# Alternating the weight chunks of the first block by unit, and a new order of the tail's additions

## The chip, the cores and the metric

The kernel runs on one core of a Trainium2 chip. The metric is the time of one execution on the device in microseconds (us). TensorE (PE in the profile) multiplies, VectorE (DVE), ScalarE (ACT) and GpSimd (POOL) work elementwise, and SyncE (SP) issues every DMA of this kernel, in order, on one queue. Each engine takes its instructions strictly in the order in which the program issues them, and waits at an instruction until its inputs and its buffer are ready.

## What is computed

```python
def _A_ref(x, dft_seq_re, dft_seq_im, dft_hid_re, dft_hid_im):
    a = jnp.einsum("bsd,ed->bse", x, dft_hid_re)
    b = jnp.einsum("bsd,ed->bse", x, dft_hid_im)
    y = jnp.einsum("ts,bse->bte", dft_seq_re, a) - jnp.einsum("ts,bse->bte", dft_seq_im, b)
    return y

def _B_ref(x, w_gate, w_up, w_down):
    g = jnp.einsum("bsd,df->bsf", x, w_gate)
    u = jnp.einsum("bsd,df->bsf", x, w_up)
    h = _gelu(g) * u
    return jnp.einsum("bsf,fd->bsd", h, w_down)

h = x + _A_ref(_layernorm(x, axis=-1), A_dft_seq_re, A_dft_seq_im, A_dft_hid_re, A_dft_hid_im)
h2 = h + _B_ref(_layernorm(h, axis=-1), B_w_gate, B_w_up, B_w_down)
```

x has 2048 rows of 448; the feed-forward part is 1792 wide. All inputs are float32.

## The kernel before

Each float32 operand is split into a high and a low float16 half (`hi_part` on ACT, `lo_part` on DVE), and a product is made of three float16 products. Large products use a seven-product scheme for 2x2 blocks: sums and differences of the blocks are formed first (by DVE or POOL), seven products are accumulated in PSUM by PE, and the results are combined ("drained") afterwards.

**Stages.** The first 345 us are the Fourier sublayer (the sequence stage, `seq_mm` and `fast_mm`, with the hidden stage `hid_mm` between). Meanwhile ten of the fourteen gate/up weight chunks are prepared (`DFT_F` gives chunk and step) and stored in DRAM (`w_dram`); the chunks 0, 1, 2 come last and stay in the three-buffer ring of weights, `w_tile`. Then come 42 units t of the gate and up products (`GateUp`), in three blocks of `NF` = 14: block 0 covers half of the rows (512 columns of the moving side per matmul), blocks 1 and 2 a quarter each (256 columns). A unit makes the products `x1`, `z1` (issued at the end of the unit before), `y1`, `x2`, `z2`, `y2`, and `y3` (issued at the start of the unit after). They collect in three PSUM banks X, Y and Z. DVE makes the results: c from Z after `z2`, one half of the hidden values hs from Y after `y2` (L1019), the other half after `y3` (L1088). `y3` goes on in the bank that `y2` has filled, so PE waits there until DVE has read it.

**Block 0** also makes what the sequence stage had no time for. Four gate/up chunks (`JIT_F`, 3 to 6 before) are made just in time, two units ahead: four additions and four low halves on DVE (`w.sums`, `w.lo`), four high halves on ACT, and a store. In units 0 to 6 the seven chunks n of w_down are prepared (`down_hi`, `down_lo`, `down_sums`): their sums on POOL, three low halves on DVE. The remaining chunks are loaded back from `w_dram` two units ahead (`gw_load`). Units 6 and later also carry side work, lists of steps with a unit and a place k in it, run by `do(t, k)`: the split and transposition of the third quarter's activations (`AT_A`) and, in block 1, of the fourth's (`AT_B`).

**Blocks 1 and 2** also run the down product for what is ready: 56 chunks d = 7 p + n (row tile p of 8, chunk n of 7), each 21 matmuls (`dn_mm`). A chunk's hidden values are loaded from DRAM two units ahead (`hid_load`, six buffers), its sums are made at the end of that unit (`dn_sums`: two operations on POOL, the fifth sum on DVE), its high and low halves in the next unit (`dn_hi`, `dn_lo`), its matmuls in the one after. Chunks of the last two row tiles (`LAST`, p = 6 and 7) cannot all be run in the units; eight of them (`EARLY`: unit and chunk) are split beforehand, in units 32 to 41, at the end of the unit. When a row tile's seven chunks are done its four banks are drained (`Drain`): ACT copies two banks to v, DVE adds parts of all four, and POOL makes eight additions (`sums`) into hr, which is stored.

**The tail**, after unit 41, runs the chunks 42 to 52 and then the last three. The chunks in `jit` (46, 47, 48, 53, 54, 55) are still to be split; step i of the loop issues the split of one and the sums of the next. Drain 5's additions were issued at i = 5, drain 6 after chunk 48. Chunk 49's seventh product uses a bank that drain 6 has to release.

Of the kernel before, what the change touches and what calls it, by code (L numbers as in the profile page):

```python
# [13 lines left out]
P = 128  # L14
# [18 lines left out]
def kernel(  # L33
# [181 lines left out]

    def down_sums(n):
        t = wd32[n]
        s = wd_s[n] = fops.tile([P, 5, HD], F32, tag="xs", name=f"wd_s_{n}")
        G.tensor_sub(s[:, 2:4], t[:, 0:2], t[:, 2:4])  # L219
        t22 = t.rearrange("p (a b) d -> p a b d", a=2)  # L220
        G.tensor_add(s[:, 0:2], t22[:, :, 0], t22[:, :, 1])
        G.tensor_add(s[:, 4], t[:, 0], t[:, 3])
# [504 lines left out]


    gu = {}
    DFT_F = ((13, 17), (12, 20), (11, 25), (10, 29), (9, 33), (8, 37), (7, 41), (0, 45), (1, 48), (2, 50))  # L730
    JIT_F = range(3, 7)

    early, after = {}, {}

# [380 lines left out]
    def gw_load(t):  # L1115
        gw[t] = w_tile(f"gw{t}")
        nc.sync.dma_start(gw[t], w_dram[f_of(t)])
# [41 lines left out]
    def dn_sums(d):  # L1159
        t = dn_hid(d)  # L1160
        if d in LAST:
            spare.append(d)
            s = fops.tile([P, 5, P], F32, tag=("xn", "tt")[len(spare) % 2], name=f"dn_s{d}")
        elif d % 4 < 2:
            s = late.tile([P, 5, P], F32, tag="dn_s", bufs=2, name=f"dn_s{d}")
        else:
            if d % 4 == 2:
                opened["s"] = prep.tile([P, 10, P], F32, tag="s", name=f"dn_s{d}")
            s = opened["s"][:, d % 4 % 2 * 5 :][:, :5]
        dn_s[d] = s  # L1170
        G.tensor_add(s[:, 0:2], t[:, 0:2], t[:, 2:4])  # L1171
        G.tensor_sub(s[:, 2:4], t[:, 1:4:2], t[:, 0:4:2])  # L1172
        V.tensor_add(s[:, 4], t[:, 0], t[:, 3])  # L1173

    def dn_parts(d):
        return (dn_hid(d)[:, 0:4:3], slice(0, 2)), (dn_s[d], slice(2, 7))
# [68 lines left out]
    for q, t0, step, when in ((2, 6, 3, AT_A), (3, 14, 6, AT_B)):  # L1245
        for j in range(2):
            plan = (
                lambda q=q, j=j: ffn_bias(q, j),
                lambda q=q, j=j: ffn_norm_act(q, j, hp[q, j]),
                lambda q=q, j=j: ffn_sums(q, j, (0,)),  # L1250
                lambda q=q, j=j: ffn_sums(q, j, (1,)),
                lambda q=q, j=j: ffn_sums(q, j, (2,)),
                lambda q=q, j=j: ffn_hi(q, j, (0,)),
                lambda q=q, j=j: ffn_sums(q, j, (3,)),
                lambda q=q, j=j: ffn_lo(q, j, (0,)),
                lambda q=q, j=j: ffn_hi(q, j, (1,)),
                lambda q=q, j=j: ffn_lo(q, j, (1,)),
                lambda q=q, j=j: ffn_lo(q, j, (2,)),
                lambda q=q, j=j: ffn_lo(q, j, (3,)),
                lambda q=q, j=j: ffn_transpose(q, j, (0,)),  # L1260
                lambda q=q, j=j: ffn_lo(q, j, (4,)),
                lambda q=q, j=j: ffn_transpose(q, j, (1, 2)),
                lambda q=q, j=j: ffn_transpose(q, j, (3,)),
            )
            for (f, k), what in zip(when, plan):
                at(side, (t0 + step * j + f, k), what)
# [8 lines left out]
    cur = GateUp(0)  # L1275
    cur.x1()
    cur.z1()
    down_load(2)
    down_load(3)
    prev = None  # L1280
    for t in range(NF):
        w = gu.get(t + 2) if t + 2 in JIT_F else None
        if t + 2 > JIT_F[-1] and t + 2 < NF:
            gw_load(t + 2)
        elif t + 2 >= NF:
            gw_load(t + 2)
        if t + 2 == NF:
            for d in (0, 1, 2):
                hid_load(d)
        if t + 1 == NF:  # L1290
            hr_load(0)
        if prev:
            prev.y3()
        if w:
            w.sums()
        cur.y1()
        if t == 3:

            gelu_table()
        if w:  # L1300
            w.hi(True)
        if t < NC:
            down_hi(t, 0)
            down_lo(t, 0)
        cur.x2()
        if t < NC:
            down_hi(t, 1)
        if w:
            w.hi(False)
            w.lo(True)  # L1310
        cur.z2()
        do(t, 1)
        cur.y2()
        do(t, 2)
        cur.c_last()
        if t == NF - 1:
            dn_hi(0)
        if t == 1:
            hid_mm(NP - 1, 0)
        prev, cur = cur, GateUp(t + 1)  # L1320
        cur.x1()
        if w:
            w.lo(False)
            gw[t + 2] = w.w
        if t < NC:
            for part in W_LO1:
                down_lo(t, 1, part)
            if t + 1 < NC:
                down_sums(t + 1)
        if t == NF - 1:  # L1330
            dn_lo(0)
        cur.z1()
        if t == 1:
            hid_mm(NP - 1, 1)
            hid_add(NP - 1, 0)
            ffn_moments(NB - 1, 1, hp[NB - 1, 1], 0)
            hid.close()
            late = ctx.enter_context(tc.tile_pool(name="late", bufs=1, reuse_waits="tile"))
            hops_tile(2)
        if t == 2:  # L1340
            hid_add(NP - 1, 1)
            ffn_moments(NB - 1, 1, hp[NB - 1, 1], 1)
            h_store(NB - 1, 1)

            sd_last = root(moments[NB - 1, 1], "h_last")
        if t == 3:
            mv = moments[NB - 1, 1]
            moments[NB - 1, 1] = mv, rstd(mv, sd_last, "h_last", const)
        if t == NF - 2:
            dn_sums(0)  # L1350
        if t == NF - 1:
            dn_sums(1)
            dn_sums(2)
        do(t, 3)
        if t > 0:
            before.store()
        before = prev
        if w:
            w.store()
        if t + 4 in JIT_F and t > 0:  # L1360
            gu[t + 4] = Weights(t + 4)
        if 1 <= t and t + 3 < NC:
            down_load(t + 3)
        do(t, 4)


# [8 lines left out]
    for t in range(NF, N_GU):  # L1375
# [12 lines left out]
            hr_load(6 + (t == N_GU - 2))  # L1388
        dn_mm(now[0], range(0, 6))
        prev.y3()  # L1390
        cur.y1()
        cur.x2()
        dn_mm(now[0], range(6, 13 if len(now) == 1 else 21))
# [2 lines left out]
        cur.z2()  # L1396
        do(t, 1)
        cur.y2()
        do(t, 2)
        cur.c_last()  # L1400
        for d in ahead[:1]:
            dn_lo(d)
# [20 lines left out]
            dn_sums(d)  # L1423
        if extra is not None:
            dn_hi(extra)
            dn_lo(extra)
        do(t, 3)
        if t == NF:
            before.store()
# [11 lines left out]
    prev.y3()  # L1441
    hid_load(47)
    prev.store()
    drain = drains[5]
    jit = [46, 47, 48, 53, 54, 55]
    for i, d in enumerate(range(6 * NC, 7 * NC + 4)):
        dn_mm(d)
        if jit:
            n = jit.pop(0)
            dn_hi(n)  # L1450
            if jit:
                dn_sums(jit[0])
            dn_lo(n)
            if len(jit) > 1:
                hid_load(jit[1])
        if i == 5:
            drain.sums(range(8))
            dn_store(5)
        if d == 7 * NC - 1:
            drain = dn_drain(6)  # L1460
            drain.copy()
            drain.bank2()
            drain.bank3()
            drain.sums(range(8))
            dn_store(6)
# [73 lines left out]
```

## Time and profile before

| what | value |
|---|---|
| median of 3 runs | 732.19 us (730.95 to 733.11) |
| profiled execution | 733.34 us, of which the span is 730.6 us |
| granted clock of PE, mean | 0.991 |
| busy: PE, DVE, ACT, POOL | 709.9, 527.6, 355.6, 207.6 us |

The span runs from the first to the last instruction; the rest of the execution lies around it. Times in the views are microseconds from the start of the span. A line such as L1213 is a line of the kernel, and a helper's line can stand for many places: tiles tell them apart. A row of the timeline gives start, duration, engine, line, operation, tiles written and read, shapes and count; a bracket at its end is the engine's idle time just before it and who ended it.

### The profile page before, as it was taken

How to read it: one execution, taken by the hardware profiler on the slowest of the kernel's cores; microseconds unless marked ns; L12 is line 12 of the kernel's file. 1: busy time of each engine (PE TensorE's matmuls, PEld its weight loads, DVE VectorE, ACT ScalarE, POOL GpSimd, SP SyncE). 2: the span in 40 equal slices, each digit the busy share in tenths (PEclk: the TensorE clock that was granted, in tenths of full speed). 3: DMA queues.
4: the chain of work that ended last, by engine and by line, in shares of the span. 5: the costliest groups of instructions: out<-in, count | busy, mean ns of one | idle time of the engine just before them, and what ended most of it. 6: DMA issues, size and time to landing. Idle time of an engine off the chain costs nothing.

```text
span 730.6 us, 13052 instructions
## 1 busy us (share of the span) xinstructions
PE 709.9 (97%) x4952; PEld 483.5 (66%) x4952; DVE 527.6 (72%) x1024; ACT 355.6 (49%) x656; POOL 207.6 (28%) x240
## 2 busy tenths in 40 slices
PE   9999999999999999999998999999999999999868
PEld 5555555555555556988443344489998999899867
DVE  7996746677669689998769654467667856889872
ACT  5775524253425355542646544355555454555420
POOL 0000000000000000001234621244565764878762
PEclk9999999999999999999999999999999999999998
DMA  8887639999979689473738658894988867788312
GB/s 265 257 246 243 149 102 289 205 294 244 287 256 261 220 254 258 144 188 119 174 119 305 198 168 205 223 293 167 297 262 259 279 213 258 276 277 285 113 58 76
DMA packets 116463, 160.47 MB, mean 220 GB/s; under 512 B 62000, under 2 KB 80560, under 8 KB 116400
## 3 DMA queue, kind: packets, MB, share of 16 engines
q1 hardware_dynamic: 116400, 159.64, 72.8%
q8 instruction: 38, 0.62, 0.3%
q14 instruction: 25, 0.20, 0.1%
HBM read 110.85 MB, written 34.87 MB: 199 GB/s over the span
## 4 chain that ended last, share of the span: by engine, by line
PE 83%; DVE 7%; POOL 4%; DMA 3%; ACT 2%; issue 1%; SPq 0%; DVEq 0%; POOLq 0%; ACTq 0%
PE acc L647 32%; PE pY L1009 12%; PE acc_d L1213 11%; PE y L713 9%; PE pZ L1009 7%; PE pX L1009 7%; PE acc_f L519 6%; DMA hid<-hid_dram 2%; POOL hr L971 2%; DVE dn_w L112 1%; DVE gu_w L114 1%; POOL dn_s L1171 1%; POOL dn_s L1172 1%; DMA hid_dram<-hs 1%; DMA wr<-in_w_seq_dram 1%
## 5 line engine op out<-in xcount | busy, mean ns | idle before, releaser
L647 PE MATMUL acc<-xs,ws 128*128 128x448 f16 x1248 | 237.9, 352 | 0.2 <-ACT ws L108 0.2
L647 PEld LDWEIGHTS <-ws 128*128 128x128 f16 x1248 | 122.0, 98 | 114.2 <-ACT ws L108 0.4
L1009 PEld LDWEIGHTS <-gw 128*128 128x128 f16 x1365 | 133.3, 98 | 44.8 <-issue 1.9
L1213 PE MATMUL acc_d<-wd,dn_w 128*128 128x224 f16 x1008 | 110.6, 259 | 0.7 <-ACT v L939 0.7
L219 POOL TENSOR_TENSOR wd_s<-wd 128x448 f32<-128x448 f32 x7 | 7.9, 1131 | 347.4 <-DVE r_h L141 342.0
L1213 PEld LDWEIGHTS <-dn_w 128*128 128x128 f16 x1008 | 96.9, 98 | 2.8 <-issue 0.9
L1009 PE MATMUL pY<-hops,gw 128*128 128x256 f16 (+1 forms) x595 | 89.2, 294 | 0.0
L1103 POOL TENSOR_TENSOR hs<-hs,c 128x256 f32<-128x256 f32 (+1 forms) x42 | 52.8, 1257 | 126.5 <-DVE hs L1019 69.1
L114 DVE SCALAR_TENSOR_TENSOR ws<-wr,ws 128x1024 f16<-128x1024 f32 (+2 forms) x66 | 75.1, 1140 | 10.4 <-ACT ws L108 10.0
L108 ACT ACTIVATE ws<-wr 128x1024 f16<-128x1024 f32 (+2 forms) x66 | 63.8, 981 | 23.1 <-DMA wr<-in_w_seq_dram 21.5
L713 PE MATMUL y<-wh,z 128*128 128x448 f16 x336 | 66.2, 352 | 0.0
L1009 PE MATMUL pZ<-hops,gw 128*128 128x256 f16 (+1 forms) x385 | 61.7, 294 | 1.5 <-DVE c L1019 1.5
L1009 PE MATMUL pX<-hops,gw 128*128 128x256 f16 (+1 forms) x385 | 61.7, 294 | 0.0
L1171 POOL TENSOR_TENSOR dn_s<-hid 128x256 f32<-128x256 f32 x56 | 48.2, 861 | 34.9 <-DMA hid<-hid_dram 31.8
L112 DVE TENSOR_TENSOR dn_w<-dn_s,dn_w 128x640 f16<-128x640 f32 x48 | 54.1, 1127 | 0.1
L1019 DVE SCALAR_TENSOR_TENSOR c<-pZ,u 128x256 f32<-128x256 f32 (+1 forms) x42 | 21.4, 509 | 44.6 <-PE pZ L1009 42.2
L713 PEld LDWEIGHTS <-z 128*128 128x128 f16 x336 | 32.9, 98 | 30.1
L1009 PEld LDWEIGHTS <-gu_w 128*128 128x128 f16 x273 | 27.0, 99 | 38.9 <-issue 8.6
L1173 DVE TENSOR_TENSOR dn_s<-hid 128x128 f32<-128x128 f32 x56 | 30.8, 565 | 27.1 <-DMA hid<-hid_dram 26.8
L519 PEld LDWEIGHTS <-ws 128*128 128x128 f16 x504 | 48.3, 98 | 0.9
L1065 ACT ACTIVATE u<-pY 128x256 f32<-128x256 f32 (+1 forms) x42 | 19.1, 454 | 59.7 <-PE pY L1009 59.7
L1172 POOL TENSOR_TENSOR dn_s<-hid 128x256 f32<-128x256 f32 x56 | 45.1, 806 | 0.0
(133 smaller groups left out, 928.4 us busy)
## 6 DMA issues: line engine op xcount, KB each, us to landing
gw<-w_dram SPq DMA_DIRECT2D x35, 896.0 KB, 5.5
wr<-in_w_seq_dram SPq DMA_DIRECT2D x100, 256.0 KB, 4.7
hid_dram<-hs SPq DMA_DIRECT2D x28, 512.0 KB, 6.6
hid<-hid_dram SPq DMA_DIRECT2D x56, 256.0 KB, 5.9
w_dram<-gu_w SPq DMA_DIRECT2D x14, 896.0 KB, 6.0
gu_raw<-in_w_gu_dram SPq DMA_DIRECT2D x28, 384.0 KB, 5.8
wr<-in_w_seq_dram SPq DMA_DIRECT2D x14, 512.0 KB, 5.2
x<-in_x_dram SPq DMA_DIRECT2D x16, 224.0 KB, 3.9
```

What stands on the lines that cost most here:

```text
L108: A.activation(dst, src, AF.Copy, scale=scale)
L112: V.tensor_sub(dst, src, hi)
L114: V.scalar_tensor_tensor(dst, src, scale, hi, op0=ALU.mult, op1=ALU.subtract)
L519: PE.matmul(fast_sum(n, k), fast_a(n, i, lw, a), fast_b(j, lx, b), start=j == 0 and m == 0 and k % 2 == 0, stop=j == NT // 2 - 1 and m == ...
L647: PE.matmul(acc[key][:, :D], w[:, lw, block * P : (block + 1) * P], xs[c][:, lx, :], start=c == 0 and m == 0, stop=c == NT - 1 and m == 2,)
L713: PE.matmul(y[:, :D], z[p][:, lz, k, g * P : (g + 1) * P], wh[:, lw, k, :], start=k == 0 and m == 0, stop=k == 6 and m == 2,)
L1009: PE.matmul(ps, w[:, wl, wa + ws, :], ops[:, m + ms, :], start=first and n == 0, stop=last and n == len(terms) - 1, skip_group_check=True,)
L1103: G.tensor_mul(c22, c22, self.cols(self.c12))
L1171: G.tensor_add(s[:, 0:2], t[:, 0:2], t[:, 2:4])
L1172: G.tensor_sub(s[:, 2:4], t[:, 1:4:2], t[:, 0:4:2])
L1173: V.tensor_add(s[:, 4], t[:, 0], t[:, 3])
L1213: PE.matmul(ps, w[:, la, a, :], wd[n][:, lb, b, :], start=n == 0 and m == 0 and opens, stop=n == NC - 1 and m == 2, skip_group_check=True,)
```

## The change

- `DFT_F`, `JIT_F`: the sequence stage prepares the chunks 13, 12, 11, 9, 7, 5, 3, 0, 1, 2 (before: 13 to 7 and 0, 1, 2), block 0 makes 4, 6, 8, 10 (before: 3 to 6), in the units 2, 4, 6, 8. Chunks 3, 5, 7, 9 and 11 to 13 are loaded back.
- `PREP_AT`: down chunk n is prepared in the units 0, 1, 3, 5, 7, 9, 11 (before: 0 to 6). Its raw loads and its sums move with it; the sums of chunks from 2 on lie in another buffer, which the down product's sums use later as one tile of two halves.
- The fifth sum of a chunk becomes `dn_sum5`, issued after `y3` in the unit of its split, and in the tail after the low half of the chunk before.
- The low half of an `EARLY` chunk is issued a unit later, after `y3`. The last of them, 52's, stands in the tail.
- `do(t, 2)` in blocks 1 and 2 moves from behind `y2` to the end of the unit; one transposition moves to the next entry of the side list.
- In the tail hid 48 is loaded ahead of the loop, 53 to 55 a step earlier, and drain 5's additions and its store stand at i = 0, behind the sums of chunk 47.

```diff
@@ -215,7 +215,8 @@
 
     def down_sums(n):
         t = wd32[n]
-        s = wd_s[n] = fops.tile([P, 5, HD], F32, tag="xs", name=f"wd_s_{n}")
+        place = (late, "dn_s") if n > 1 else (fops, "xs")
+        s = wd_s[n] = place[0].tile([P, 5, HD], F32, tag=place[1], name=f"wd_s_{n}")
         G.tensor_sub(s[:, 2:4], t[:, 0:2], t[:, 2:4])
         t22 = t.rearrange("p (a b) d -> p a b d", a=2)
         G.tensor_add(s[:, 0:2], t22[:, :, 0], t22[:, :, 1])
@@ -727,8 +728,8 @@
 
 
     gu = {}
-    DFT_F = ((13, 17), (12, 20), (11, 25), (10, 29), (9, 33), (8, 37), (7, 41), (0, 45), (1, 48), (2, 50))
-    JIT_F = range(3, 7)
+    DFT_F = ((13, 17), (12, 20), (11, 25), (9, 29), (7, 33), (5, 37), (3, 41), (0, 45), (1, 48), (2, 50))
+    JIT_F = range(4, 11, 2)
 
     early, after = {}, {}
 
@@ -1162,7 +1163,9 @@
             spare.append(d)
             s = fops.tile([P, 5, P], F32, tag=("xn", "tt")[len(spare) % 2], name=f"dn_s{d}")
         elif d % 4 < 2:
-            s = late.tile([P, 5, P], F32, tag="dn_s", bufs=2, name=f"dn_s{d}")
+            if d % 4 == 0:
+                opened["l"] = late.tile([P, 10, P], F32, tag="dn_s", name=f"dn_s{d}")
+            s = opened["l"][:, d % 4 * 5 :][:, :5]
         else:
             if d % 4 == 2:
                 opened["s"] = prep.tile([P, 10, P], F32, tag="s", name=f"dn_s{d}")
@@ -1170,7 +1173,10 @@
         dn_s[d] = s
         G.tensor_add(s[:, 0:2], t[:, 0:2], t[:, 2:4])
         G.tensor_sub(s[:, 2:4], t[:, 1:4:2], t[:, 0:4:2])
-        V.tensor_add(s[:, 4], t[:, 0], t[:, 3])
+
+    def dn_sum5(d):
+        t = dn_hid(d)
+        V.tensor_add(dn_s[d][:, 4], t[:, 0], t[:, 3])
 
     def dn_parts(d):
         return (dn_hid(d)[:, 0:4:3], slice(0, 2)), (dn_s[d], slice(2, 7))
@@ -1259,8 +1265,8 @@
                 lambda q=q, j=j: ffn_lo(q, j, (3,)),
                 lambda q=q, j=j: ffn_transpose(q, j, (0,)),
                 lambda q=q, j=j: ffn_lo(q, j, (4,)),
-                lambda q=q, j=j: ffn_transpose(q, j, (1, 2)),
-                lambda q=q, j=j: ffn_transpose(q, j, (3,)),
+                lambda q=q, j=j: ffn_transpose(q, j, (1,)),
+                lambda q=q, j=j: ffn_transpose(q, j, (2, 3)),
             )
             for (f, k), what in zip(when, plan):
                 at(side, (t0 + step * j + f, k), what)
@@ -1275,14 +1281,12 @@
     cur = GateUp(0)
     cur.x1()
     cur.z1()
-    down_load(2)
-    down_load(3)
     prev = None
+    PREP_AT = {0: 0, 1: 1, 3: 2, 5: 3, 7: 4, 9: 5, 11: 6}
     for t in range(NF):
         w = gu.get(t + 2) if t + 2 in JIT_F else None
-        if t + 2 > JIT_F[-1] and t + 2 < NF:
-            gw_load(t + 2)
-        elif t + 2 >= NF:
+        n = PREP_AT.get(t)
+        if t > 0 and w is None:
             gw_load(t + 2)
         if t + 2 == NF:
             for d in (0, 1, 2):
@@ -1293,18 +1297,20 @@
             prev.y3()
         if w:
             w.sums()
+        if t == NF - 1:
+            dn_sum5(0)
         cur.y1()
         if t == 3:
 
             gelu_table()
         if w:
             w.hi(True)
-        if t < NC:
-            down_hi(t, 0)
-            down_lo(t, 0)
+        if n is not None:
+            down_hi(n, 0)
+            down_lo(n, 0)
         cur.x2()
-        if t < NC:
-            down_hi(t, 1)
+        if n is not None:
+            down_hi(n, 1)
         if w:
             w.hi(False)
             w.lo(True)
@@ -1322,11 +1328,13 @@
         if w:
             w.lo(False)
             gw[t + 2] = w.w
-        if t < NC:
+        if n is not None:
             for part in W_LO1:
-                down_lo(t, 1, part)
-            if t + 1 < NC:
-                down_sums(t + 1)
+                down_lo(n, 1, part)
+        if t + 1 in PREP_AT and t > 0:
+            down_sums(PREP_AT[t + 1])
+        if t == 0:
+            down_sums(1)
         if t == NF - 1:
             dn_lo(0)
         cur.z1()
@@ -1357,10 +1365,10 @@
         before = prev
         if w:
             w.store()
-        if t + 4 in JIT_F and t > 0:
-            gu[t + 4] = Weights(t + 4)
-        if 1 <= t and t + 3 < NC:
-            down_load(t + 3)
+        if w and w.f + 4 in JIT_F:
+            gu[w.f + 4] = Weights(w.f + 4)
+        if n is not None and 2 <= n + 2 < NC:
+            down_load(n + 2)
         do(t, 4)
 
 
@@ -1388,6 +1396,12 @@
             hr_load(6 + (t == N_GU - 2))
         dn_mm(now[0], range(0, 6))
         prev.y3()
+        for d in ahead:
+            dn_sum5(d)
+        if t - 1 in EARLY:
+            dn_lo(EARLY[t - 1])
+        if t in EARLY:
+            dn_sum5(EARLY[t])
         cur.y1()
         cur.x2()
         dn_mm(now[0], range(6, 13 if len(now) == 1 else 21))
@@ -1396,7 +1410,6 @@
         cur.z2()
         do(t, 1)
         cur.y2()
-        do(t, 2)
         cur.c_last()
         for d in ahead[:1]:
             dn_lo(d)
@@ -1423,7 +1436,7 @@
             dn_sums(d)
         if extra is not None:
             dn_hi(extra)
-            dn_lo(extra)
+        do(t, 2)
         do(t, 3)
         if t == NF:
             before.store()
@@ -1441,6 +1454,9 @@
     prev.y3()
     hid_load(47)
     prev.store()
+    hid_load(48)
+    dn_sum5(46)
+    dn_lo(52)
     drain = drains[5]
     jit = [46, 47, 48, 53, 54, 55]
     for i, d in enumerate(range(6 * NC, 7 * NC + 4)):
@@ -1451,11 +1467,13 @@
             if jit:
                 dn_sums(jit[0])
             dn_lo(n)
-            if len(jit) > 1:
-                hid_load(jit[1])
-        if i == 5:
-            drain.sums(range(8))
-            dn_store(5)
+            if jit:
+                dn_sum5(jit[0])
+            if len(jit) > 2:
+                hid_load(jit[2])
+            if i == 0:
+                drain.sums(range(8))
+                dn_store(5)
         if d == 7 * NC - 1:
             drain = dn_drain(6)
             drain.copy()
```

## The prediction

> **What bounds the kernel now.** I read the page first, then TensorE's own waits, then the timeline around each of those waits. The page:
>
> ```profile
> span 730.6 us, 13052 instructions
> PE 709.9 (97%) x4952; PEld 483.5 (66%) x4952; DVE 527.6 (72%) x1024; ACT 355.6 (49%) x656; POOL 207.6 (28%) x240
> ```
>
> PE is busy for 97% of the span and the change touches no matmul, so all that can be won lies in PE's few idle stretches and in slowed matmuls right behind them. The waits of PE (total, times, longest):
>
> ```profile
> PE acc_d L1213 <- ACT v L939: 7.0, 2, 6.3
> PE pY L1009 <- DVE hs L1019: 4.5, 2, 2.9
> PE acc_d L1213 <- DVE hs L1088: 2.0, 1, 2.0
> PE pZ L1009 <- DVE c L1019: 1.5, 2, 1.3
> ```
>
> That is 15.0 us, nearly all in six places. The timeline has them; the bracket is PE's idle time just before the row:
>
> ```profile
> 391.91 2.53 PE L1009 MATMUL pY<-hops,gu_w 128*128 128x512 f16 x11 [1.56 <-DVE hs L1019]
> 403.43 4.22 PE L1009 MATMUL pY<-hops,gu_w 128*128 128x512 f16 x11 [2.94 <-DVE hs L1019]
> 552.15 0.73 PE L1213 MATMUL acc_d<-wd,dn_w 128*128 128x224 f16 x6 [0.72 <-ACT v L939]
> 625.72 0.82 PE L1009 MATMUL pZ<-hops,gw 128*128 128x256 f16 x6 [1.30 <-DVE c L1019]
> 689.79 3.95 PE L1213 MATMUL acc_d<-wd,hops 128*128 128x224 f16 x24 [2.03 <-DVE hs L1088]
> 712.00 0.72 PE L1213 MATMUL acc_d<-wd,hops 128*128 128x224 f16 x3 [6.30 <-ACT v L939]
> ```
>
> Two lie in the first block, two in the middle, two in the tail. Three of them cost more than the idle time. Windows of the trace behind them (length, PE busy, weight loads, DVE, ACT, POOL, granted clock):
>
> ```profile
> 403.80:407.20 3.40, 3.40 (x10) 1.22 (x8) 2.68 (x5) 0.64 (x2) 3.40 (x2) 0.51 0.57 226
> 690.50:694.00 3.50, 3.50 (x22) 2.88 (x20) 1.46 (x2) 0.74 (x1) 0.44 (x1) 0.51 0.41 154
> 711.00:714.40 3.40, 2.40 (x14) 1.94 (x14) 0.00 (x0) 1.09 (x2) 3.32 (x6) 0.51 0.25 95
> 714.40:717.90 3.50, 3.50 (x22) 2.87 (x19) 0.00 (x0) 0.00 (x0) 3.24 (x6) 0.51 0.10 39
> ```
>
> After the idle stretches of 2.94, 2.03 and 6.30 us the clock was 0.51 for one, one and two windows of 3.4 us; a busy window at 0.51 loses 3.4 x 0.49 = 1.7 us. After 1.56 and 1.30 us I find no such window.
>
> **Part one, the first block.** A unit there takes PE 430.53 - 422.11 = 8.42 us (chain of waits, start and length):
>
> ```profile
> 422.11 2.37 PE pY L1009 x11
> 430.53 2.37 PE pY L1009 x11
> ```
>
> DVE's work for it stands in windows over 346 to 407 us of tile gu_s (four units' gate/up sums and their low halves: DVE, then ACT), of tile wd (five down chunks: PE, DVE, ACT, POOL), and in DVE's groups by form:
>
> ```profile
> 346.00:407.00 61.00, 16.27 (x24) 4.68 (x8) 0.97 0.61 191
> 346.00:407.00 61.00, 0.00 (x0) 11.10 (x15) 8.49 (x10) 12.35 (x14) 0.97 0.61 191
> L114 DVE SCALAR_TENSOR_TENSOR gu_w<-gu_raw,gu_w 128x512 f16<-128x512 f32 x4 | 2.7, 682 | 0.0
> L114 DVE SCALAR_TENSOR_TENSOR gu_w<-gu_raw,gu_w 128x256 f16<-128x256 f32 x4 | 1.7, 416 | 0.0
> L1019 DVE SCALAR_TENSOR_TENSOR c<-pZ,u 128x512 f32<-128x512 f32 x14 | 9.6, 689 | 20.9 <-PE pZ L1009 20.9
> ```
>
> A gate/up chunk costs DVE 16.27/4 + 0.68 + 0.42 = 5.17 us, a down chunk 11.10/5 = 2.22, the unit's own three results 3 x 0.69 = 2.07. With both chunks that is 9.46 us against 8.42: DVE falls back by about 1 us per unit, and by units 3 and 4 the second result (hs L1019) comes too late for the matmuls that go on in its bank. After the change no unit has both: 5.17 + 2.07 = 7.24 or 2.22 + 2.07 = 4.29 us. Nothing else is late next: units 6 to 12 also carry the split of the third quarter's activations, which now meets gate/up chunks 8 and 10, but in the one unit that has most of it (8) this is a few short instructions, and the result that PE needs stands ahead of them in DVE's queue. So both stalls and the slow window go: 1.56 + 2.94 + 1.7 = **6.2 us**. The work is not less, only spread. What was covered and may come out: weights 3 and 5 now come back from memory where 3 and 5 were made on the spot. Seven such loads stand in the block before and after, but the one for unit 5 joins the thickest traffic. From the page and the windows (the last two columns are the DMA share and GB/s):
>
> ```profile
> gw<-w_dram SPq DMA_DIRECT2D x35, 896.0 KB, 5.5
> 387.60:397.70 10.10, 8.54 (x40) 3.79 (x39) 9.34 (x16) 7.90 (x16) 3.56 (x3) 1.00 1.04 359
> ```
>
> It is issued on SP near 386, behind stores of hidden values, of h and of weights and behind a raw load, and lands after 5.5 us at the median. Unit 5's first matmuls come near 396 without the stalls (403.43 - 2.94 - 1.56 = 398.9, less two products of 1.3). If it stood last of all that this window moved, it would land at 397.7, 1.7 us late. I take nothing, the median being nearer, and keep 0 to 1.7 us.
>
> **Part two, the middle.** The two smaller stalls and what stood ahead of them:
>
> ```profile
> 550.29 1.08 ACT L108 ACTIVATE xs<-tt 128x768 f16<-128x768 f32 x2
> 622.58 0.29 DVE L1173 TENSOR_TENSOR dn_s<-hid 128x128 f32<-128x128 f32 x1 [1.33 <-DMA hid<-hid_dram]
> 622.78 0.95 DVE L112 TENSOR_TENSOR hops<-hid,hops 128x256 f16<-128x256 f32 x1
> 623.66 1.34 DVE L112 TENSOR_TENSOR hops<-dn_s,hops 128x640 f16<-128x640 f32 x1
> ```
>
> At 552 the drain's copy was behind 1.08 us of activation halves on ACT; the second side list now stands at the unit's end, behind the copy, so 0.72 us goes. At 625 DVE first sat 1.33 us for a transfer that its fifth addition needed, then did 0.95 + 1.34 us of an early chunk's low half, and only then the results that PE waited for. Now the results of the last matmuls come first, then the additions of chunks that have long landed, the low half, and the addition that may wait. The same work still stands ahead of c, but the 1.33 us of waiting gets filled: I take 1.0 of the 1.30. Sum **1.7 us**. Bounds: 0 (all of it comes back at another unit) to 2.0. The later low half holds a hid buffer longer, so one load (chunk 45's) goes out some 2 us later on SP; its sums come third in POOL's row there, so I cost it at nothing.
>
> **Part three, the tail.** It is the hard part. Rows of the timeline:
>
> ```profile
> 685.20 1.61 DVE L943 SCALAR_TENSOR_TENSOR hr<-acc_d,hr 128x224 f32<-128x224 f32 x4
> 668.92 4.04 POOL L971 TENSOR_TENSOR hr<-hr,v 128x224 f32<-128x224 f32 x4
> 689.48 0.73 POOL L1171 TENSOR_TENSOR dn_s<-hid 128x256 f32<-128x256 f32 x1 [0.76 <-DVE dn_xs L112]
> 697.77 6.20 PE L1213 MATMUL acc_d<-wd,dn_w 128*128 128x224 f16 x63
> 697.27 0.83 POOL L1171 TENSOR_TENSOR dn_s<-hid 128x256 f32<-128x256 f32 x1 [6.33 <-DMA hid<-hid_dram]
> 698.08 0.90 POOL L1172 TENSOR_TENSOR dn_s<-hid 128x256 f32<-128x256 f32 x1
> 699.01 0.74 ACT L108 ACTIVATE dn_w<-dn_s 128x640 f16<-128x640 f32 x1 [1.43 <-POOL dn_s L1172]
> 706.38 0.74 ACT L108 ACTIVATE dn_w<-dn_s 128x640 f16<-128x640 f32 x1 [1.01 <-POOL dn_s L1172]
> 706.31 11.33 POOL L971 TENSOR_TENSOR hr<-hr,v 128x224 f32<-128x224 f32 x16
> 711.41 0.54 ACT L939 ACTIVATE v<-acc_d 128x448 f32<-128x448 f32 x1 [4.29 <-POOL hr L971]
> 712.00 15.37 PE acc_d L1213 x129
> ```
>
> Before, POOL idles 6.33 us up to 697.27, does the sums of chunks 48, 53, 54, 55, and only from 706.31 drain 5's eight additions; ACT's copy of drain 6 waits for six of them until 711.41, PE until 712.00. On the same clock the new order runs so (to read against the rows):
>
> - The last result (hs L1088, for which PE waited until 689.79) no longer queues behind chunk 52's low half and follows the drain's additions, near 687.6. PE's 2.03 us there and the slow window at 690.5 go. PE then takes 2.0 us per chunk and is through 47 near 698.
> - DVE: fifth addition, then 52's low half (0.95 + 1.34): done near 690.2. POOL's sums of 47 share its buffer and wait for it, as at 689.48: 690.2 + 0.83 + 0.90 = 691.9.
> - Drain 5's eight additions now: the first six took 706.31 to 711.41, 0.85 us each, so 6.8 us: 698.7. Alone the later ones took (11.33 - 5.1)/10 = 0.62; four beside DVE's low halves 4.04, 1.01 each.
> - **What is late next** is chunk 48: its sums stand behind them on POOL, 698.7 + 1.73 = 700.4, then ACT and DVE, 0.74 + 1.34: 702.5. PE wants it at 698.5 and stops some 4 us. A second wait follows: drain 6's copy stands on ACT behind the high halves of 53, 54, 55. From the half of 48 to that of 55 it was 706.38 - 699.01 = 7.37 us, as DVE has 2.3 us of low half for each. So 700.4 + 7.4 + 0.74 = 708.5, and PE goes on 0.6 us later, 709.1 instead of 712.0: **2.9 us**.
> - From there the same 129 matmuls, 15.37 us with two slow windows behind the stall. At 2.0 us per 21 they are 12.3 us. With stalls of about 4 and 3.6 us instead of one of 6.3 I leave the slow windows as they are.
> - SP: the store of drain 5 waits for POOL and holds back the loads of 54 and 55; with 700 and a landing of 3 to 6 us they come when POOL reaches them or up to 3 us later. I take nothing.
>
> Bounds of the tail: additions at 1.01 give 1.3 us less, 1.6 us; the loads late by 3 us give 0. Additions at 0.62 (5.0 us) let PE go on at 707.3, and with full clock it ends 12.3 us later at 719.6 instead of 727.4: 7.8 us.
>
> **The sum.** 6.2 + 1.7 + 2.9 = 10.8 us. The profiled execution took 733.34 us (span 730.6 and 2.7 around it), so its like would take 722.5. It stands 1.15 us above the median of 732.19, so the median goes to **721.4 us**.
>
> The Trainium skill, "TensorE: Matmul & The Clock Gate", Part 1: The HAM clock gate, says that the clock halves after at least one idle window of about 3.4 us. By that, the stalls of 2.94 and 2.03 us would cost no clock and the sum would be 9.1 us, 723.1; the rows at 403.8 and 690.5 say otherwise, so I keep 1.7 for the first.
>
> **Rivals.**
>
> - *The tail is freed*: the 7.8 us of the upper bound, and chunks 53 to 55 at PE's own 2.0 us each instead of 7.37 / 3, 1.4 more: 6.2 + 1.7 + 9.2 = 17.1, 715.1 us. For: POOL had 6.33 idle us. Against: 0.95 and 1.34 us for low halves beside POOL.
> - *Transfers and POOL eat part of it*: unit 5's weights 1.7 us late, the middle 0, the tail 1.6: 4.5 + 1.6 = 6.1, 726.1 us. For: DMA share 1.04 there.
> - *The change doesn't do what it says*: the late hs in the first block is held by its buffer's store, not by DVE's load; then 6.2 stays, 4.6 is left, 727.6 us. Against: both rows of the stall name DVE, which worked without a pause there.
> - *Slower*: early chunks' low halves (2.29 us) stand ahead of the result c in seven units (33, 34, 36, 38 to 41), and PE waits for c in each as at 625. At 1.30 us each, 9.1, it takes the other 9.1 us back; from 1.6 us each it is slower beyond what a measurement of this kernel can tell (0.3%, 2.2 us), and at 2.03 each, 14.2 us, the time is 732.2 - 9.1 + 14.2 = 737.3. Against: before, the same instructions stood ahead of c, and one unit stalled by over 1 us.
>
> **Chances.** Forecast (719 to 724) 0.58; tail freed 0.15; part eaten 0.15; not what it says 0.05; slower mechanism 0.07, of which 0.04 beyond 0.3%. Something between forecast and no change may also land within 0.3%. So faster 0.90, same 0.06, slower 0.04. The range runs from the freed tail, 715.0, to 727.6.
>
> **What would show it.** Right: no PE idle before pY in units 3 and 4 and clock 1.00 at 390 to 410; no wait for hs L1088 at the start of the tail; POOL's eight additions before 48's sums; PE stalls at chunk 48 and at 49's seventh product, the latter behind ACT's high half of 55. Wrong: PE waits for gw in unit 5, for c in units 33 to 41, or no stall at 48 at all.

## The result, and the profile after

The changed kernel takes 719.82 us (median of 4 runs, 717.73 to 720.45) against 732.28 us (4 runs, 730.95 to 733.11) before: ratio 0.9827, 95% interval 0.9800 to 0.9853. Of the changed kernel's four runs the profiled one is the fastest, 717.73 us, and the only one with a granted clock of 1.000; the other three had 0.998, about one slow window of 3.4 us, and spans of 717.4 to 718.6 us. Its span is 14.6 us shorter than the span before (730.6 us), some 2 us more than the medians differ by.

The page and the waits of PE (total, times, longest), after the change:

```profile
span 716.0 us, 13066 instructions
PE 704.2 (98%) x4952; PEld 480.7 (67%) x4952; DVE 522.1 (73%) x1024; ACT 355.5 (50%) x656; POOL 201.9 (28%) x240
...
PE acc_d L1219 <- ACT v L940: 3.1, 1, 3.1
PE acc_d L1219 <- DVE dn_w L112: 2.3, 2, 1.4
...
PE pZ L1010 <- DVE c L1020: 1.2, 3, 0.6
```

The 4.5 us of pY on hs and the 2.0 us of hs at the tail's start are gone; the drain's copy costs 3.1 instead of 7.0. New is a wait of 1.4 us on a low half. The timeline of PE has these places:

```profile
389.55 1.24 PE L1010 MATMUL pY<-hops,gw 128*128 128x512 f16 x5
...
397.97 1.24 PE L1010 MATMUL pY<-hops,gu_w 128*128 128x512 f16 x5
...
481.00 0.56 PE L1219 MATMUL acc_d<-wd,dn_w 128*128 128x224 f16 x4 [1.40 <-DVE dn_w L112]
...
545.30 0.74 PE L1219 MATMUL acc_d<-wd,dn_w 128*128 128x224 f16 x6
...
618.21 0.82 PE L1010 MATMUL pZ<-hops,gw 128*128 128x256 f16 x6 [0.63 <-DVE c L1020]
...
692.73 0.37 PE L1219 MATMUL acc_d<-wd,dn_w 128*128 128x224 f16 x2 [0.40 <-ACT dn_w L108]
694.00 1.42 PE L1219 MATMUL acc_d<-wd,dn_w 128*128 128x224 f16 x13 [0.91 <-DVE dn_w L112]
...
700.22 0.45 PE L1219 MATMUL acc_d<-wd,hops 128*128 128x224 f16 x3 [3.08 <-ACT v L940]
```

Rows without a bracket had no wait. Both kernels issue 4952 matmuls of the same shapes in the same order, so the start of one matmul can be compared with its start before, and the change of that difference from place to place says where the 14.6 us between the two spans came from:

| matmul, start before and after | ahead by | since the row above |
|---|---|---|
| before the block, 349.41 and 348.99 | 0.42 | |
| end of the slow window in the block, 407.27 and 400.12 | 7.15 | +6.73: stalls 1.72 and 3.10, clock 1.69, rest 0.22 |
| start of block 1, 486.58 and 481.00 | 5.58 | −1.57: the new wait |
| drain 4's bank, 552.15 and 545.30 | 6.85 | +1.27 |
| c, 625.72 and 618.21 | 7.51 | +0.66 |
| last units, 678.50 and 672.17 | 6.33 | −1.18: waits for c and small ones |
| start of the tail, 689.79 and 681.23 | 8.56 | +2.22: no wait for hs |
| behind its slow window, 693.90 and 683.73 | 10.18 | +1.62: clock |
| chunk 48, 702.57 and 694.00 | 8.56 | −1.62: two waits |
| chunk 49's seventh product, 712.00 and 700.22 | 11.78 | +3.22: shorter wait |
| last matmuls, 727.10 and 712.49 | 14.61 | +2.83: clock |

That is 6.7 us from the block, −1.6 behind it, +0.7 from the middle and 8.3 from the tail. The first 0.42 us stand ahead of the block and are in none of these parts: at 349 us PE waits for ACT, 0.70 us before, not at all in this trace, and up to 1.10 us in others. That no slow window follows the tail's stall is seen in the windows (length, PE busy, weight loads, DVE, ACT, POOL, granted clock), two in the block and two behind the wait of 3.08 us:

```profile
389.60:393.00 3.40, 3.40 (x17) 1.52 (x16) 3.30 (x10) 1.41 (x3) 0.26 (x1) 1.00 1.09 403
397.97:401.40 3.43, 3.43 (x17) 1.55 (x16) 1.29 (x2) 1.40 (x3) 3.29 (x4) 1.00 0.63 207
...
700.20:703.60 3.40, 3.38 (x36) 3.37 (x36) 1.78 (x5) 0.41 (x1) 3.27 (x5) 1.00 0.00 0
703.60:707.00 3.40, 3.40 (x38) 3.40 (x36) 0.00 (x0) 0.00 (x0) 1.96 (x4) 1.00 0.14 54
```

The clock is 1.00 in all four, where three of the corresponding four before had 0.51.

### The profile page after: what moved, and what is told of

Read it like the earlier page. It is cut to its first block, busy times and chain, and to the rows that moved or that the text cites. A ratio compares the mean times of both kernels' runs of the same rounds, so it can differ in the third digit from the quotient of the medians.

```text
span 716.0 us, 13066 instructions
## 1 busy us (share of the span) xinstructions
PE 704.2 (98%) x4952; PEld 480.7 (67%) x4952; DVE 522.1 (73%) x1024; ACT 355.5 (50%) x656; POOL 201.9 (28%) x240
## 4 chain that ended last, share of the span: by engine, by line
PE 92%; DVE 4%; POOL 1%; DMA 1%; issue 1%; ACT 0%; SPq 0%; ACTq 0%; POOLq 0%; DVEq 0%
PE acc L648 33%; PE pY L1010 13%; PE acc_d L1219 12%; PE y L714 9%; PE pX L1010 9%; PE pZ L1010 9%; PE acc_f L520 7%; DVE dn_w L112 1%; DMA hid_dram<-hs 1%; DVE dn_s L1179 1%; POOL hr L972 1%; PE pw L102 1%; DVE dn_l L112 0%; ACT dn_w L108 0%; DVE hr L944 0%
## 5 line engine op out<-in xcount | busy, mean ns | idle before, releaser
L220 POOL TENSOR_TENSOR wd_s<-wd 128x448 f32<-128x448 f32 x7 | 9.5, 1352 | 343.4 <-DMA wd<-in_w_down_dram 342.6
L1104 POOL TENSOR_TENSOR hs<-hs,c 128x256 f32<-128x256 f32 (+1 forms) x42 | 47.5, 1131 | 127.6 <-DVE hs L1020 64.4
L1174 POOL TENSOR_TENSOR dn_s<-hid 128x256 f32<-128x256 f32 x56 | 45.4, 812 | 29.2 <-DMA hid<-hid_dram 27.9
L1175 POOL TENSOR_TENSOR dn_s<-hid 128x256 f32<-128x256 f32 x56 | 46.2, 826 | 0.0
L108 ACT ACTIVATE dn_w<-dn_s 128x640 f16<-128x640 f32 x48 | 35.1, 730 | 21.4 <-DVE dn_s L1179 10.1
L1089 DVE SCALAR_TENSOR_TENSOR hs<-pY,g 128x256 f32<-128x256 f32 (+1 forms) x42 | 21.3, 506 | 33.5 <-PE pY L1010 33.0
```

The lines of the kernel that those rows point to most:

```text
L108: A.activation(dst, src, AF.Copy, scale=scale)
L1089: V.scalar_tensor_tensor(h, y, SC, g, op0=ALU.mult, op1=ALU.mult)
L1104: G.tensor_mul(c22, c22, self.cols(self.c12))
```

## The experiments

Times are medians; ratios are to the kernel before in the same series of runs, whose medians were 731.44, 731.56 and 731.74 us.

**The block alone.** The weight chunks alternate as in the change; the order of the units and of the tail is that of before. (This edit and all that follow are shown against the changed kernel, shortened; `...` marks what is left out.)

```diff
-        V.tensor_add(dn_s[d][:, 4], t[:, 0], t[:, 3])
+        V.tensor_add(s[:, 4], t[:, 0], t[:, 3])
...
-        if t - 1 in EARLY:
-            dn_lo(EARLY[t - 1])
...
+        do(t, 2)
         cur.c_last()
...
-    hid_load(48)
...
+        if i == 5:
+            drain.sums(range(8))
+            dn_store(5)
```

> The first block's alternation alone, everything after it in the order of before. Theory A (DVE's overload made the two stalls of units 3 and 4; the tail is a matter of its own): PE has no wait in units 3 and 4 and no slow clock window behind them, 6.7 us ahead of before at the end of the block; a new wait of about 1.4 us at the first down chunk of block 1, as in the changed kernel, takes some back; the waits of 1.3, 2.0 and 6.3 us later stay as they were. So 5 us less than before: 727 us. Rival B (the stalls moved, not removed: PE's gain in the block is lost again where POOL or transfers bound the later stages): 730 us or more.

It took 728.44 us, ratio 0.9964 (0.9945 to 0.9984). Against before, PE is 0.64 us behind at the start of the block and 6.08 ahead at its end: the block gains 6.72 us, as in the full change (6.73), near the 6.2 forecast. PE then loses 1.64 at block 1's start, as the full change does, and 0.76 where the drain's bank is needed:

```profile
548.48 0.73 PE L1216 MATMUL acc_d<-wd,dn_w 128*128 128x224 f16 x6 [1.58 <-ACT v L940]
...
694.04 0.84 POOL L1174 TENSOR_TENSOR dn_s<-hid 128x256 f32<-128x256 f32 x1 [6.63 <-DMA hid<-hid_dram]
...
703.14 0.74 ACT L108 ACTIVATE dn_w<-dn_s 128x640 f16<-128x640 f32 x1 [1.40 <-POOL dn_s L1175]
703.07 11.34 POOL L972 TENSOR_TENSOR hr<-hr,v 128x224 f32<-128x224 f32 x16
...
708.18 0.54 ACT L940 ACTIVATE v<-acc_d 128x448 f32<-128x448 f32 x1 [4.30 <-POOL hr L972]
```

The middle's wait is larger than before (1.58 for 0.72 us), and the tail is as before: POOL idles 6.63 us for chunk 48, the additions start at 703.07, and the copy comes 4.30 us after the row of splits is done. The median lies between theory A's 727 us and rival B's 730: in the trace PE is 3.90 us ahead at its last matmul, so a good part of the block's gain is kept and the rest is lost in the later stages.

**The change with drain 5's additions late**, at i = 5 again.

```diff
-            if i == 0:
-                drain.sums(range(8))
-                dn_store(5)
+        if i == 5:
+            drain.sums(range(8))
+            dn_store(5)
```

> The changed kernel with drain 5's eight additions and its store back at step 5 of the tail; they stand behind the sums of 55 on POOL again. Theory A (what binds at the end is the row of splits 48, 53, 54, 55 on DVE and ACT, with drain 6's copy behind it, and the additions hardly count): the wait at chunk 48 (2.7 us in the changed kernel) goes, the copy is free some 0.6 us later than in the changed kernel, PE waits 5 to 6 us at chunk 49's seventh product in place of 3.1, and one or two slow clock windows follow: 0.6 us plus 0 to 3.4, so 720.5 to 724 us. Rival B (moving the additions is what freed the tail): PE waits there 8 us or more, 725 us or more.

721.38 us, ratio 0.9868 (0.9846 to 0.9891). There is no wait at chunk 48 and one of 6.46 us at chunk 49; PE goes on at 702.16, 1.94 us later than in the change, and at a slow clock. The tail's rows:

```profile
696.41 11.39 POOL L972 TENSOR_TENSOR hr<-hr,v 128x224 f32<-128x224 f32 x16
...
697.88 0.74 ACT L108 ACTIVATE dn_w<-dn_s 128x640 f16<-128x640 f32 x1 [1.77 <-DVE dn_s L1179]
701.57 0.55 ACT L940 ACTIVATE v<-acc_d 128x448 f32<-128x448 f32 x1 [2.94 <-POOL hr L972]
```

The time lies in theory A's range, but not for its reason: the row of splits is done at 698.62, and the copy then waits 2.94 us for POOL's additions. Without the early additions the tail is already better than the block's alone: chunk 48's load is early, POOL no longer idles for it, and its row of sums ends at 696.4 instead of 703.1.

**The block and the early additions**, without the rest.

```diff
-        if i == 5:
+        if i == 0:
             drain.sums(range(8))
+        if i == 5:
             dn_store(5)
```

> The first block's alternation with drain 5's additions at step 0 of the tail (the store left at step 5), all else in the order of before. Theory A (POOL's additions cost PE about 1.6 us when late, and the rest of the tail's gain comes from DVE's order): 1 to 3 us less than the block alone, 726 to 727.5 us, with the wait of 1.9 us at the tail's start and a wait at chunk 48 and at 49. Rival B (the additions' place is the tail's gain): 723 us or less.

722.06 us, ratio 0.9849 (0.9813 to 0.9884). By medians that is 6.4 us from one moved line, where the line's absence in the run above costs 1.6. The four runs spread from 718.70 to 724.32 us; in the traces PE's lead over before grows by 5.8 us from the tail's start to the last matmul, and by 0.4 in the block alone. The theory of 1 to 3 us fell. PE waits 1.88 us for hs at the tail's start, 0.44 and 0.28 at chunk 48, 2.29 at 49. The middle's wait is there as in the block alone:

```profile
548.13 1.28 PE L1216 MATMUL acc_d<-wd,dn_w 128*128 128x224 f16 x6 [1.59 <-ACT v L940]
```

**Down chunk 6 a unit earlier**, to find the cause of the new wait at block 1's start.

```diff
-    PREP_AT = {0: 0, 1: 1, 3: 2, 5: 3, 7: 4, 9: 5, 11: 6}
+    PREP_AT = {0: 0, 1: 1, 3: 2, 5: 3, 7: 4, 9: 5, 10: 6}
```

> The changed kernel with down chunk 6 prepared in unit 10 in place of unit 11. Theory A (the new wait of 1.4 us at the start of block 1 comes from chunk 6's low halves ahead of the activations' low halves in unit 11, which delay the transpositions on SP, these the store of unit 12's hidden values, and that the buffer of unit 14): the first transposition of the last group is issued 1 to 2 us earlier against PE, DVE's wait for the store (2.9 us) shrinks to under 1.5 us and PE's wait of 1.4 us goes: about 1.5 us less, 718.3 us. Rival B (the transpositions themselves got slower, 8.7 against 8.2 us for three, from traffic): the wait stays, no change.

717.86 us, ratio 0.9824 (0.9803 to 0.9845); the wait is gone. The ratio is that of the change (0.9827), so the time itself does not show a gain; the evidence is in the traces. The rows are first those of the change, then those of this run, in the same order of steps:

```profile
455.11 2.46 DVE L114 SCALAR_TENSOR_TENSOR wd<-wd_s,wd 128x448 f16<-128x448 f32 x2
457.49 0.95 DVE L112 TENSOR_TENSOR xs<-tt,xs 128x768 f16<-128x768 f32 x1
...
458.46 1.26 SPq L306 DMA_TRANSPOSE hops<-xs  x1
...
462.70 8.74 SPq L306 DMA_TRANSPOSE hops<-xs  x3
...
472.65 0.54 SPq L1110 DMA_DIRECT2D hid_dram<-hs  x1
...
480.19 0.42 DVE L1020 SCALAR_TENSOR_TENSOR hs<-pY,m 128x256 f32<-128x256 f32 x1 [2.91 <-DMA hid_dram<-hs]
```

```profile
456.27 0.95 DVE L112 TENSOR_TENSOR xs<-tt,xs 128x768 f16<-128x768 f32 x1
...
457.25 1.26 SPq L306 DMA_TRANSPOSE hops<-xs  x1
...
462.19 8.54 SPq L306 DMA_TRANSPOSE hops<-xs  x3
...
471.93 0.54 SPq L1110 DMA_DIRECT2D hid_dram<-hs  x1
...
479.47 0.42 DVE L1020 SCALAR_TENSOR_TENSOR hs<-pY,m 128x256 f32<-128x256 f32 x1 [1.03 <-DMA hid_dram<-hs]
```

In the change the last low halves of down chunk 6 (2.46 us) stand on DVE ahead of the low halves of the activations. The transpositions, which need those, are issued later on SP, and behind them the store of a unit's hidden values. DVE wants that tile's buffer in block 1's first unit and goes on 7.54 us after the store's issue in both runs (480.19 − 472.65 and 479.47 − 471.93). Behind that waiting instruction stands the low half for which PE waits 1.40 us. PE's matmuls up to there come 1.17 us later in this run than in the change (5.98 us ahead of before, not 7.15); against PE, then, the store is issued 0.72 + 1.17 = 1.89 us earlier, and that is what DVE's wait lost (2.91 − 1.03).

**Drain 6's copy ahead of the splits of 54 and 55**, which go behind it; nothing else is changed.

```diff
-        if jit:
+        if i < 4:
...
+        elif i == 4:
+            dn_sums(55)
+            dn_sum5(55)
+        elif i in (7, 8):
+            n = jit.pop(0)
+            dn_hi(n)
+            dn_lo(n)
```

> The changed kernel with the splits of chunks 54 and 55 issued behind drain 6's copy (steps 7 and 8 of the tail), their sums ahead of it. Theory A (PE waits 3.1 us at chunk 49's seventh product because the copy stands on ACT behind 55's high half): that wait goes, 2.5 to 3.1 us less, 717 us. Rival B (POOL's additions hold v until then): the wait stays. Rival C (54 and 55 then come too late for the last row tile): a wait of about the same size appears before the last 63 matmuls, no change.

715.23 us, ratio 0.9783 (0.9763 to 0.9803). ACT's rows, those of the change first (48's half, 55's half, the copy), then those of this run:

```profile
691.93 0.74 ACT L108 ACTIVATE dn_w<-dn_s 128x640 f16<-128x640 f32 x1 [4.61 <-POOL dn_s L1175]
...
699.00 0.74 ACT L108 ACTIVATE dn_w<-dn_s 128x640 f16<-128x640 f32 x1 [1.29 <-DVE dn_s L1179]
699.65 0.96 ACT L940 ACTIVATE v<-acc_d 128x448 f32<-128x448 f32 x2
```

```profile
691.35 0.74 ACT L108 ACTIVATE dn_w<-dn_s 128x640 f16<-128x640 f32 x1 [4.61 <-POOL dn_s L1175]
...
693.66 0.74 ACT L108 ACTIVATE dn_w<-dn_s 128x640 f16<-128x640 f32 x1 [1.26 <-DVE dn_s L1179]
694.30 0.96 ACT L940 ACTIVATE v<-acc_d 128x448 f32<-128x448 f32 x2
695.15 0.42 ACT L108 ACTIVATE dn_w<-hid 128x256 f16<-128x256 f32 x1
```

The copy starts 2.95 us behind 48's half (694.30 − 691.35) instead of 7.72, and the 3.08 us wait is gone: the copy's place behind 55's high half was what held PE. The medians differ by 4.6 us, more than that wait; the granted clock is 1.000 in all four runs, so the slow window of 1.7 us that three of the change's four runs seem to have had is missing as well. The wait at block 1's start is missing in this profile too, though nothing there was changed: the three transpositions took 7.34 us instead of 8.74. So the wait depends on that length too, which varies from one execution to the next. Of the eight traces with chunk 6 in unit 11, six show 1.2 to 1.6 us, one 0.6 and this one none; the three with it in unit 10 show none.

**Both of the last two**, and then **the tail laid out anew** on top of both: drain 5's additions behind the sums of 48, its store a step later still, all three of 53 to 55 split behind drain 6's copy, and drain 6's additions behind their sums.

```diff
-            if i == 0:
+            if i == 1:
                 drain.sums(range(8))
+            if i == 2:
                 dn_store(5)
...
+        if i in (6, 7):
+            n = jit.pop(0)
+            dn_hi(n)
+            dn_sums(jit[0])
+            dn_lo(n)
+            dn_sum5(jit[0])
...
```

> Both single improvements together on the changed kernel: the splits of 54 and 55 behind drain 6's copy, and down chunk 6 in unit 10. Theory A (the two waits are independent): the wait at 49's seventh product stays away, as with the copy first alone (715.2 us), and DVE's wait for the store at the start of block 1 stays at about 1 us in place of 1.6 to 3.0, so PE never waits there: 714 to 715 us, with less spread. Rival B (the wait at block 1's start is chance from execution to execution): 715.2 us as with the copy first alone.

> As the run before, and in the tail: drain 5's additions behind the sums of 48, drain 6's copy ahead of the splits of 53, 54 and 55, drain 6's additions behind their sums. Theory A (chunk 48 waits because its sums stand behind the eight additions on POOL): the wait of 1.3 us at 48 goes as well, 1 to 1.4 us less than the run before, 713 to 714 us. Rival B (then DVE, with three low halves of 2.3 us behind the drain, is too late for the last 63 matmuls): a wait of 1 to 3 us before or in the last row tile, no gain or worse.

Both together took 713.90 us, ratio 0.9760 (0.9740 to 0.9780), which overlaps the interval of the copy first alone. The new layout took 712.55 us (5 runs), ratio 0.9750 (0.9726 to 0.9774), the fastest of all, though its interval overlaps that of the other. Its waits are:

```profile
PE pw L102 <- POOL sign_t L93: 1.4, 1, 1.4
PE pZ L1010 <- DVE c L1020: 1.2, 3, 0.7
PE pY L1010 <- ACT pY L1055: 1.1, 1, 1.1
```

The tail has none left.

**Early chunks' low halves in their own unit**, as before.

```diff
-        if t - 1 in EARLY:
-            dn_lo(EARLY[t - 1])
...
             dn_hi(extra)
+            dn_lo(extra)
...
-    dn_lo(52)
```

> The changed kernel with the low halves of the early chunks back at the end of their own unit. Theory A (they stand ahead of DVE's last result hs and of c, as before): PE waits 2.0 us at the start of the tail again with a slow clock window behind, and up to 1.3 us in the middle near 618; what follows in the tail starts later by that: 721.5 to 724 us. Rival B (moving the fifth additions alone did it; the place of the low halves is nothing): no change, 719.8 us.

719.12 us, ratio 0.9834 (0.9814 to 0.9853), no different from the change. The wait for hs at the tail's start is back,

```profile
683.02 2.46 PE L1219 MATMUL acc_d<-wd,hops 128*128 128x224 f16 x24 [1.29 <-DVE hs L1089]
```

but PE is held again at chunks 48 (0.34 us) and 49 (3.06), and the median loses nothing that can be measured.

**The second side list back behind y2.**

```diff
         cur.y2()
+        do(t, 2)
         cur.c_last()
...
-        do(t, 2)
```

> The changed kernel with the second side list back behind y2, ahead of the drain's copy on ACT. Theory A: PE waits 0.7 us again near 545 for the copy of a drain; nothing else moves: 0.7 us more, 720.5 us. Rival B (another order of ACT's work hides it by now): no change, 719.8 us.

719.89 us, ratio 0.9847 (0.9825 to 0.9870). The drain's wait, 0.72 us before, did not come back beyond 0.2 us. The wait at chunk 49 is the change's own, 3.07 us, but here the window behind it had half the clock:

```profile
697.40:700.90 3.50, 0.58 (x6) 0.54 (x6) 2.97 (x6) 2.01 (x5) 1.28 (x2) 0.97 0.00 0
700.90:704.30 3.40, 3.40 (x22) 2.81 (x20) 1.18 (x4) 0.00 (x0) 3.32 (x6) 0.53 0.00 0
```

**The fifth addition back with the sums.**

```diff
         G.tensor_sub(s[:, 2:4], t[:, 1:4:2], t[:, 0:4:2])
+        V.tensor_add(s[:, 4], t[:, 0], t[:, 3])
...
     def dn_sum5(d):
-        t = dn_hid(d)
-        V.tensor_add(dn_s[d][:, 4], t[:, 0], t[:, 3])
+        pass
```

> The changed kernel with the fifth additions back in the sums at the end of a unit, where DVE meets them while their transfers are under way; the low halves of early chunks stay a unit later. Theory A (the place of the fifth additions removed the waits of the middle, and lets DVE come to its last result hs and so to chunk 48's transfer early): PE waits 0.7 us or more near 545 and at 620, about 1 to 2 us at the start of the tail, since DVE sits for chunk 46's transfer ahead of hs, and the later waits move by as much: 722 to 725 us. Rival B (the order on ACT and the additions' place on POOL did it all): no change, 719.8 us.

717.53 us, ratio 0.9799 (0.9770 to 0.9828). The theory that waits return here fell: DVE again waits for transfers, but the drain's bank costs PE nothing, the wait for c grows only from 0.63 to 1.02 us, and that at chunk 49 falls from 3.08 to 2.69. It may be a little faster than the change; the intervals overlap, and this stays open.

## Why the prediction was right, and where it was wrong

The forecast was 721.4 us and the range 715.0 to 727.6; the time is 719.82. By medians the gain is 12.5 us for 10.8 forecast. The parts fit less well than the sum. In the profiled execution the block gave 0.5 us more than forecast and the tail 5.4 more, the middle 1.0 less, and block 1's start lost 1.6 that were not forecast. That the median came within 1.6 us of the forecast is partly luck: these errors have both signs, and about 2 us of the profile's gain are not in the median.

- **The block**: 6.2 forecast, 6.7 measured in the change and with the block alone. Both stalls and the slow window went once no unit held both chunks, as forecast. The size given for DVE's load, about 1 us too much per unit, is not enough for stalls of 1.56 and 2.94 us, since DVE had caught up as late as 374.42, where it waited 6.09 us for PE. Nor did it work quite without a pause: it waited 0.73 us for ACT at 389.10. And from hs of unit 3 to hs of unit 4 it took 402.69 − 391.18 = 11.51 us, not 9.46: 2.94 of them (395.36 to 398.30) are statistics of some rows, which the sum left out. One of these instructions took 1.12 us before and 0.16 us in the change:

```profile
395.55 1.12 DVE L142 TENSOR_TENSOR r_h_last<-r_h_last 128x2 f32<-128x2 f32 x1
...
390.68 0.16 DVE L142 TENSOR_TENSOR r_h_last<-r_h_last 128x2 f32<-128x2 f32 x1
```

Before, POOL was making sums of a down chunk at that time (from 395.52), and in the change it was idle from 389.85 to 396.53. That this made the difference is likely, not shown. The reserve for unit 5's weights was not needed: the matmuls on gw near 395 have no wait.
- **"Nothing else is late next"** is the step that failed, at −1.57 us. The prediction looked at what PE needs from DVE in those units, and there it was right. It did not follow the moved low halves past the split of the activations to SP, whose queue holds transpositions of 8.74 us and a store behind them. Moving chunk 6 by one unit shows it: the wait is in seven of eight traces with the chunk in unit 11, and in none of three with it in unit 10.
- **The middle**: 1.7 forecast, 0.7 measured. The 0.72 us went, but the reason given, ACT's halves of the activations ahead of the copy, is not the whole of it. Before, ACT also idled 0.90 us for a chunk's sums just ahead of those halves:

```profile
549.64 0.74 ACT L108 ACTIVATE dn_w<-dn_s 128x640 f16<-128x640 f32 x1 [0.90 <-POOL dn_s L1172]
```

In the two runs with the old order of both the side list and the fifth additions (and of one transposition) the wait is 1.58 and 1.59 us; with either one alone in the old order it is not there. So either change suffices. The term "1.0 of the 1.30" was too large: 0.63 us is left, and 0.39 and 0.16 appear at two later units; the early low half still stands ahead of c.
- **The tail**: 2.9 forecast, 8.3 in the profile. The chain was named rightly: additions, chunk 48's sums, row of splits, drain 6's copy behind 55's high half. The sizes were too cautious. POOL's rows of the change:

```profile
684.52 6.02 POOL L972 TENSOR_TENSOR hr<-hr,v 128x224 f32<-128x224 f32 x8
690.50 0.72 POOL L1174 TENSOR_TENSOR dn_s<-hid 128x256 f32<-128x256 f32 x1
691.18 0.72 POOL L1175 TENSOR_TENSOR dn_s<-hid 128x256 f32<-128x256 f32 x1
```

Just ahead of the tail PE is 6.33 us ahead, so on the prediction's clock the sums of 47 end at 690.9 (forecast 691.9), the eight additions take 6.0 us (6.8), 48's sums end at 698.2 (700.4), and the splits from 48 to 55 take 699.00 − 691.93 = 7.07 us (7.37). PE goes on at 700.22 + 6.33 = 706.6, not 709.1: these terms make 2.5 us. Chunk 48 cost PE 0.40 + 0.91 us, not about 4. The step "I leave the slow windows as they are" failed as well: none followed in this execution, 2.8 us. That was luck, as the last section shows, and part of it is missing in the median: the clock of 0.998 in the other three runs fits one slow window each. A term taken at nothing was not quite nothing: POOL waited 1.06 us for the load of chunk 54 (at 694.33).

- **What made the tail's gain.** The early additions and the other steps of the tail (chunk 48's load, the order on DVE) are largely two ways to the same thing, since drain 6's copy waits both for v, which POOL must have read, and for ACT's row of splits. From the block alone (728.4 us) the additions alone give 6.4 us, all other steps without them 7.1, and both together 8.6, so whichever comes second is worth 1.6 or 2.2. These two are not clear of the noise: the intervals of the ratios overlap with that of the change.
- **The rivals.** PE did wait for c in the later units, which the prediction had named as a sign of being wrong, but only 0.63 + 0.39 + 0.16 = 1.2 us in all, not 1.3 in each of seven units, and the run with those low halves in their own unit is no faster. The freed tail was priced at 9.2 us; the profiled execution came near it (8.3) for want of slow windows, with PE still held at 48 and 49, and the median did not. The new layout, without those waits, reached 712.55 us.
- **The clock rule.** The Trainium skill, "TensorE: Matmul & The Clock Gate", Part 1, lets the clock halve after at least one idle window of about 3.4 us. The traces disagree: a stall of 2.94 us cost 1.69 us of clock before, which the change won back, and one of 2.03 us was followed by a slow window too. The prediction was right to go by its own rows.

## What to carry to other kernels

Follow a moved instruction past its own engine: the few us on DVE did no harm there, but delayed a transposition on the DMA queue, a store behind it, and a buffer a unit later. Where two things end last at nearly the same time, undo each alone and both together before giving either a price. A copy that frees a bank should stand ahead of work that is only wanted later: here this removed a wait of 3.1 us, and the median went from 719.8 to 715.2 us.

## What was not expected of the hardware

- Idle stretches of nearly one length (3.07 and 3.08 us, at the same matmul) were followed by a slow window of 3.4 us in two traces (0.53 and 0.50) and by none in two, while stretches of 2.03 and 2.94 us were followed by one. So the length alone does not decide. The traces show what does. Within a trace all changes of the granted clock lie whole multiples of 3.413 us apart; before, it turned slow at 403.84, 690.56 and 711.04 us, which is 84 and 6 such steps. Counting PE's idle time in each step between two such points separates the cases (length, PE busy, weight loads, DVE, ACT, POOL, granted clock; two steps before, then the two of the change that share the stall of 3.08 us):

```profile
687.14:690.56 3.42, 1.39 (x16) 1.23 (x14) 3.42 (x6) 1.40 (x4) 2.66 (x4) 1.00 0.01 4
704.21:707.62 3.41, 1.49 (x16) 1.33 (x14) 3.38 (x5) 1.89 (x4) 2.97 (x4) 1.00 0.02 5
...
695.47:698.88 3.41, 1.68 (x18) 1.52 (x16) 3.41 (x6) 1.46 (x3) 2.56 (x3) 1.00 0.04 7
698.88:702.30 3.42, 2.08 (x22) 2.07 (x22) 2.57 (x7) 1.60 (x3) 1.97 (x3) 1.00 0.00 0
```

PE idled 2.03 us in the first of these steps, and the next step was slow; it idled 1.92 us in the second, and the next was not. In the change a point of this grid falls inside the stall and divides it into 1.73 and 1.34 us: no slow window. With the side list back 3.05 us of a stall of 3.07 fall into one step, and the next is slow. In the eleven traces that record a change of the clock, take every full-speed step between the first and the last matmul: those with 2.03 us of idle time or more (nine) were all followed by a slow one, those with 1.92 us or less never. The ends of matmuls are modelled, so the border is not exact, and no run shifted a stall alone. But where a stall falls on this grid, which lies differently in each trace, can decide over a slow window of 1.7 us.
- A store's buffer came free 7.5 us after its issue behind transpositions (7.54, 7.54 and 7.58 us in three traces), not far from the median landing of all such stores in the change (7.1 us). Three transpositions held the queue for 7.34 to 8.74 us with the same data.
